# First pair of a token block: the two parts of a step's activation in neighbouring steps, and half of M1's passes behind the second product

## Chip, cores and metric

The kernel runs on one core of a Trainium2 chip. The metric is device microseconds of one execution; the time of the kernel before is the median of three runs. The core's engines work through queues of their own, each in the order in which it is written, and wait for each other by semaphores: TensorE (PE, with its weight loads PEld), VectorE (DVE), ScalarE (ACT), GpSimd (POOL) and SyncE (SP), which issues all DMAs here.

## What is computed

An attention over channels (256 by 256 scores, summed over 6016 tokens), then two feed-forward blocks, all in float32:

```python
def _attn_ref(q, k, v, tau):
    qn = q / (np.linalg.norm(q, axis=1, keepdims=True) + 1e-06)
    kn = k / (np.linalg.norm(k, axis=1, keepdims=True) + 1e-06)
    s = kn.transpose(0, 2, 1) @ qn / tau
    s = s - s.max(-1, keepdims=True)
    a = np.exp(s)
    a /= a.sum(-1, keepdims=True) + 1e-09
    return (v @ a).astype(np.float32)

def _moe_ref(x, w_in, w_out):          # d_model 256, d_ff 2048
    h = x @ w_in
    g = h * np.clip(h + 3.0, 0.0, 6.0) / 6.0
    return g @ w_out

def _moe2_ref(x, w_in, w_out):
    r = np.maximum(x @ w_in, 0.0)
    return (r * r) @ w_out
```

The weights come as 64-bit floats and are turned into float32 on the chip.

## The kernel before

**Precision.** A float32 operand is split into a high part (rounded to TensorE's fast float32 type, a cast on ScalarE, L124) and a low part (what is left, a subtraction on VectorE, L126; in places on GpSimd). A product is three passes: high by high, low by high, high by low. `split` does both parts, or one of them with `part` 0 or 1.

**Stages.** First the scores, norms and softmax. The attention is folded into the first feed-forward's weights: M1 is the attention matrix times w_in, made in four parts (c4, "part", 0 to 3) of 512 columns. Then come the tokens in six blocks ("pairs" of up to 512 columns each) through both feed-forwards. The first pair of the first feed-forward, `(0, 0)`, runs while weights are still being converted and M1 is still being made; it is written as 32 steps in plain products. All other pairs use a Strassen scheme planned by places (`strassen`, `prepare`, `at`, `extra`, `run`); the change doesn't touch them.

**A step of the first pair.** Step k is a token half n and a 128-wide slice f of the hidden layer, the list `steps`. TensorE makes tile h (six matmuls, `whole_product`, L311), ScalarE makes r = relu(h + 3) (L651), VectorE makes g = min(r, 6) * h (L653), ScalarE casts the high part gs of g (L124), VectorE makes its low part (L126), and TensorE adds the second product to the accumulators acc (six matmuls, `second_both`, L676): four use the high part, the last two the low part. `LAG` = 2: the second product of step k is written two steps later (`pending`, `drain`). The h tiles and M1's tiles mp take turns in four banks of PSUM (`bank`), so an h or mp tile waits for the g of the tile four turns back. Tile r and tile g have two buffers each, gs has four.

**What else goes through these queues.** `issue`, called inside `first` and at the end of a step, writes a stage of a weight's conversion (`unit`, `from_float64`: L155 and L158 on ScalarE, L159, L162 and L167 on VectorE, then `split`, whose cast and subtraction are L124 and L126 as well). Every eight steps a part of M1 is made: `m1_whole` (two halves i, six passes each, tile mp), in step 8p-3 for part p = 1, 2, 3. In step 8p-2 `m1_out` takes the halves out of PSUM as high parts (three instructions of L493 on ScalarE) and low parts (three of L495 on VectorE), which are the weights wa and a21 that h of step 8p is the first to use, and `m1_keep` copies both halves for sums that GpSimd makes later (L216, then L126 on GpSimd for parts 0 and 1). In step 8p-1 the second product of step 8p-3 is written ahead of h of step 8p (`late_products`), so that the weights have longer. GpSimd also makes combinations of the next pair's tokens (L752, L759).

**Order.** The code runs under `manual_schedule`: each engine's queue is in the order in which the code writes its instructions. So the order of lines in the loop over `steps` is the order in the queues.

Of the kernel before, what the change touches and what calls it, by code (L numbers as in the profile page):

```python
# [12 lines left out]
AF = mybir.ActivationFunctionType  # L13
ALU = mybir.AluOpType
# [7 lines left out]
KC = C // P  # L22
# [8 lines left out]
LAG = 2  # L31
# [25 lines left out]
def attention_then_two_ffns(  # L57
# [30 lines left out]
    nc = tc.nc  # L88
# [13 lines left out]
    def bank(shape, name, tag=None):  # L102

        if tag is None:
            tag = "yxyq"[turn[0] % 4]
            turn[0] += 1
        return ps_h.tile(shape, F32, tag=tag, name=name, bufs=2 if tag == "y" else 1)
# [6 lines left out]
    three = const.tile([P, 1], F32, name="three")  # L114
# [3 lines left out]
    def f32(x):  # L118
        return x.bitcast(F32)

    def split(hi, lo, x, part=2, eng=nc.vector):

        if part != 1:
            nc.scalar.copy(hi, x)  # L124
        if part != 0:
            eng.tensor_tensor(out=lo, in0=x, in1=f32(hi), op=ALU.subtract)  # L126
# [198 lines left out]
    with tc.manual_schedule():  # L325
# [10 lines left out]
        for gi, n in enumerate(GROUPS):  # L336
            src = wpool.tile([P, 1024], F32, tag=f"wo{gi % NU}", name=f"qk{gi}")[:, :2 * n * C]
            nc.sync.dma_start(
                out=src.rearrange("p (t x c) -> p t x c", t=n, x=2), in_=qk[:, t:t + n, :, :]
# [5 lines left out]
            if gi == TAU_AT:  # L345
# [4 lines left out]
                    out=tq[:, 2:4], in0=tq[:, 2:4], scalar1=tau_sb, scalar2=1.0, op0=ALU.mult, op1=ALU.mult  # L350
# [119 lines left out]
        def m1_whole(c4, i):  # L470
            mps[c4, i] = bank([P, 512], f"mp{c4}_{i}")
            low_last(mps[c4, i], [
                ([t[:, j, :] for t in wi1[c4]], [t[:, i, j * P:(j + 1) * P] for t in et]) for j in range(KC)
            ], False)
# [138 lines left out]
        def tmp(tag, w, name, **kw):  # L613
            return hpool.tile([P, WMAX], F32, tag=tag, name=name, **kw)[:, :w]

        def g_tile(w, name):
            t = gpool.tile([P, 2, WMAX], F32R, tag="g", name=name)[:, :, :w]
            return [t[:, i, :] for i in range(2)]


        w0 = WIDTHS[0]
        steps = [(n, f) for f in range(KF) for n in range(2)]
        steps[:4] = [(0, 0), (0, 1), (1, 0), (1, 1)]
        hs = {}
        pending = []
# [8 lines left out]
        def product(at, k):  # L634
            if at < len(steps):
                n, f = steps[at]
                if k == 0:
                    hs[at] = bank([P, WMAX], f"h0_{n}_{f}")[:, :w0]
                passes(hs[at], [(weight0(f, k), x0[k, n])], k == 0, k == KC - 1)

        def whole_product(at):
            if at < len(steps):
                n, f = steps[at]
                hs[at] = bank([P, WMAX], f"h0_{n}_{f}")[:, :w0]
                low_last(hs[at], [(weight0(f, k), x0[k, n]) for k in range(KC)])

        def first(at_step, between):
            n, f = steps[at_step]
            h = hs.pop(at_step)
            r = tmp("r", w0, f"r0_{n}_{f}")  # L650
            nc.scalar.activation(r, h, AF.Relu, bias=three)  # L651
            g = tmp("g32", w0, f"g0_{n}_{f}")
            nc.vector.scalar_tensor_tensor(out=g, in0=r, scalar=6.0, in1=h, op0=ALU.min, op1=ALU.mult)  # L653
            between()
            gs = g_tile(w0, f"gs0_{n}_{f}")
            if at_step == len(steps) - 1:
                at(1.6, lambda: split(*gs, g, 0))
                at(3.0, lambda: split(*gs, g, 1))
            else:
                split(*gs, g)  # L660
            return gs

        def second(n, f, gs):
            return [
# [16 lines left out]
        def drain(limit):  # L681
            while len(pending) > limit:
                second_both(*pending.pop(0))
# [9 lines left out]
        def issue():  # L693
            for k, st in sorted(plan.get(place[0], ())):
                loaded[k][st]()
                if st == 4:
                    feed()
            place[0] += 1
# [4 lines left out]
        def at(place, go):  # L703
            events.append((place, len(events), go))
# [12 lines left out]
        def run(until):  # L717
            events.sort(key=lambda e: e[:2])
            while events and events[0][0] < until:
                events.pop(0)[2]()  # L720
# [210 lines left out]
        for kk in range(KC):  # L931
            for a in range(2):
                product(a, kk)
        for a, (n, f) in enumerate(steps):
            gs = first(a, issue)
            pending.append((n, f, gs))

            part, since = divmod(a + M1_LEAD, 8)
            if 0 < part < 4 and since == 1:
                for i in range(KC):  # L940
                    m1_out(part, i)
                m1_keep(part)
            late_products = (a + 1) % 8 == 0 and a < 24
            if late_products:
                drain(LAG)
            if a:
                whole_product(a + 1)
            if 0 < part < 4 and since == 0:
                for i in range(KC):
                    m1_whole(part, i)  # L950
            drain(LAG)
            issue()

            run(-(len(steps) - 1 - a) * SLOTS / 4)


        for x, go in zip(LEFT_AT, [(n, f, d, gs) for n, f, gs in pending for d in range(KC)], strict=True):
            n, f, d, gs = go
# [48 lines left out]
```

## Time and profile before

| | |
|---|---|
| median of 3 runs | 1042.24 us (1042.06 to 1043.7) |
| profiled execution, its device time | 1042.34 us |
| its span | 1040.6 us |
| TensorE busy | 1031.6 us (99%), 4630 matmuls |
| VectorE busy | 852.5 us (82%) |
| ScalarE busy | 665.0 us (64%) |
| GpSimd busy | 28.9 us (3%) |

Matmuls are pipelined: one of 512 columns is listed with 0.39 us, though the next starts 0.23 us after it. So busy time says little of TensorE; what it loses is read from the distance between starts. The loop over the 32 steps begins at about 58 us of the span. In a listing a tile's name stands without its buffer number, `out<-in`; h is a first product of the first pair, mp a half of a part of M1, acc with L676 a second product of the first pair.

### The profile page before, as it was taken

How to read it: one execution, taken by the hardware profiler on the slowest of the kernel's cores; microseconds unless marked ns; L12 is line 12 of the kernel's file. 1: busy time of each engine (PE TensorE's matmuls, PEld its weight loads, DVE VectorE, ACT ScalarE, POOL GpSimd, SP SyncE). 2: the span in 40 equal slices, each digit the busy share in tenths (PEclk: the TensorE clock that was granted, in tenths of full speed). 3: DMA queues.
4: the chain of work that ended last, by engine and by line, in shares of the span. 5: the costliest groups of instructions: out<-in, count | busy, mean ns of one | idle time of the engine just before them, and what ended most of it. 6: DMA issues, size and time to landing. Idle time of an engine off the chain costs nothing.

```text
span 1040.6 us, 12968 instructions
## 1 busy us (share of the span) xinstructions
PE 1031.6 (99%) x4630; PEld 866.4 (83%) x4630; DVE 852.5 (82%) x1429; ACT 665.0 (64%) x1200; POOL 28.9 (3%) x33
## 2 busy tenths in 40 slices
PE   9999999999999999999999999999999999999998
PEld 8878788888888888888998888888888888888997
DVE  7898868889989889988988688688688688778765
ACT  6787777787788778877876445445445455445443
POOL 0012240000000000000000000000000000000000
PEclk9999999999999999999999999999999999999999
DMA  9911204003403403212755002002001100200100
GB/s 368 349 41 43 79 3 140 1 1 117 157 1 116 157 1 117 97 56 96 254 197 187 1 1 81 1 1 80 2 1 45 37 1 3 74 1 1 41 1 36
DMA packets 25936, 77.64 MB, mean 75 GB/s; under 512 B 2832, under 2 KB 4880, under 8 KB 25872
## 3 DMA queue, kind: packets, MB, share of 16 engines
q1 hardware_dynamic: 25872, 76.82, 20.9%
q8 instruction: 36, 0.59, 0.2%
q14 instruction: 28, 0.23, 0.1%
HBM read 52.95 MB, written 23.86 MB: 74 GB/s over the span
## 4 chain that ended last, share of the span: by engine, by line
PE 90%; DVE 3%; ACT 3%; DMA 2%; issue 1%; POOL 0%; ACTq 0%; SPq 0%; POOLq 0%
PE acc L323 15%; PE acc L321 15%; PE acc L322 15%; PE y L322 8%; PE y L321 8%; PE y L323 8%; PE q L321 4%; PE q L322 4%; PE q L323 4%; PE acc L676 2%; PE h L311 2%; PE x L321 2%; PE x L323 2%; PE x L322 2%; DMA qk<-in_qk 2%
## 5 line engine op out<-in xcount | busy, mean ns | idle before, releaser
L126 DVE TENSOR_TENSOR gs<-g,gs 128x512 fp32r<-128x512 f32 (+1 forms) x384 | 260.7, 679 | 59.8 <-ACT gs L828 47.8
L323 PE MATMUL acc<-gs,wo 128*128 128x512 f32 (+1 forms) x708 | 272.5, 385 | 0.1
L322 PE MATMUL acc<-gs,wo 128*128 128x512 f32 (+1 forms) x708 | 272.5, 385 | 0.0
L321 PE MATMUL acc<-gs,wo 128*128 128x512 f32 (+1 forms) x708 | 272.4, 385 | 0.0
L828 ACT CAST gs<-g 128x512 fp32r<-128x512 f32 (+1 forms) x352 | 208.1, 613 | 27.7 <-DVE g L819 19.0
L323 PEld LDWEIGHTS acc<-gs,wo 128*128 128x128 f32 x708 | 132.9, 188 | 25.3 <-DVE gs L126 0.5
L321 PEld LDWEIGHTS acc<-gs,wo 128*128 128x128 f32 x708 | 132.9, 188 | 24.4
L322 PEld LDWEIGHTS acc<-gs,wo 128*128 128x128 f32 x708 | 132.9, 188 | 24.3
L801 ACT COPY se<-y 128x512 f32<-128x512 f32 (+1 forms) x88 | 50.8, 577 | 124.0 <-PE y L323 123.9
L805 DVE TENSOR_TENSOR h<-q,se 128x512 f32<-128x512 f32 (+1 forms) x88 | 59.6, 678 | 65.6 <-ACT se L801 65.1
L801 ACT COPY su<-y 128x512 f32<-128x512 f32 (+1 forms) x88 | 50.9, 578 | 87.0 <-PE y L323 76.1
L824 DVE SCALAR_TENSOR_TENSOR g<-h 128x512 f32<-128x512 f32 (+1 forms) x144 | 97.0, 674 | 0.0
L811 ACT ACTIVATE r<-h,three 128x512 f32<-128x512 f32 (+1 forms) x120 | 85.5, 713 | 7.9 <-DVE h L805 7.7
L819 DVE SCALAR_TENSOR_TENSOR g<-r,h 128x512 f32<-128x512 f32 (+1 forms) x120 | 80.9, 674 | 3.9 <-ACT r L811 3.8
L813 ACT ACTIVATE r<-y 128x512 f32<-128x512 f32 (+1 forms) x48 | 28.3, 589 | 62.3 <-PE y L323 62.3
L805 DVE TENSOR_TENSOR h<-q,su 128x512 f32<-128x512 f32 (+1 forms) x88 | 59.5, 676 | 1.6
L805 DVE TENSOR_TENSOR h<-x,sa 128x512 f32<-128x512 f32 (+1 forms) x88 | 59.2, 673 | 0.0
L801 ACT COPY sa<-y 128x512 f32<-128x512 f32 (+1 forms) x88 | 50.8, 577 | 6.6 <-PE y L323 0.4
L824 DVE SCALAR_TENSOR_TENSOR g<-y,r 128x512 f32<-128x512 f32 (+1 forms) x48 | 32.7, 681 | 23.2 <-ACT r L813 22.7
L676 PE MATMUL acc<-gs,wo 128*128 128x512 f32 x180 | 45.5, 391 | 1.0 <-ACT gs L124 1.0
L300 PE MATMUL s<-qk 128*128 128x256 f32 x188 | 42.0, 385 | 0.0
L676 PEld LDWEIGHTS acc<-gs,wo 128*128 128x128 f32 x180 | 33.5, 188 | 9.1 <-ACT gs L124 2.2
(247 smaller groups left out, 1801.1 us busy)
## 6 DMA issues: line engine op xcount, KB each, us to landing
qk<-in_qk SPq DMA_DIRECT2D x23, 512.0 KB, 7.4
wo<-in_w_out SPq DMA_DIRECT2D x16, 512.0 KB, 5.1
wi<-in_w_in SPq DMA_DIRECT2D x10, 512.0 KB, 4.6
x2d<-o SPq DMA_DIRECT2D x20, 256.0 KB, 2.4
raw<-x2d SPq DMA_DIRECT2D x10, 512.0 KB, 5.8
out<-o SPq DMA_DIRECT2D x20, 256.0 KB, 2.2
raw<-in_vt SPq DMA_DIRECT2D x8, 512.0 KB, 5.9
wo2d<-wo2s SPq DMA_DIRECT2D x8, 512.0 KB, 2.9
```

Source lines behind the costliest of these rows:

```text
L126: eng.tensor_tensor(out=lo, in0=x, in1=f32(hi), op=ALU.subtract)
L300: nc.tensor.matmul(s_ps[i], lhsT=x[:, C + i * P:C + (i + 1) * P], rhs=x[:, :C], start=(t == 0), stop=(t == NT - 1))
L321: nc.tensor.matmul(ps, lhsT=ah, rhs=bh, start=first, stop=False, skip_group_check=more)
L322: nc.tensor.matmul(ps, lhsT=al, rhs=bh, start=False, stop=False, skip_group_check=more)
L323: nc.tensor.matmul(ps, lhsT=ah, rhs=bl, start=False, stop=last, skip_group_check=more)
L676: nc.tensor.matmul(acc[0, 0, n, d], lhsT=wo1[u][:, i, at + d * P:at + (d + 1) * P], rhs=gs[k], start=f == 0 and (i, k) == (0, 0), stop=f = ...
L801: nc.scalar.copy(s[tag], s["y"])
L805: nc.vector.tensor_tensor(out=s[which], in0=s[ps], in1=s[tag], op=ALU.add)
L811: nc.scalar.activation(s["r" + which], h, AF.Relu, bias=three)
L819: nc.vector.scalar_tensor_tensor(out=g, in0=s["r" + which], scalar=6.0, in1=h, op0=ALU.min, op1=ALU.mult)
L824: nc.vector.scalar_tensor_tensor(out=g, in0=h, scalar=0.0, in1=r, op0=ALU.max, op1=ALU.mult)
L828: nc.scalar.copy(gs[which][0], s["g" + which])
```

## The change

Four things, all in the loop over `steps`:

- r of step k+1 is written in step k, behind that step's new product and ahead of everything else that ScalarE does in step k (`relu0`). In the steps with `late_products` it is written behind the high part of step k.
- the product of step k+1 is written at the head of step k (it stood behind the step's r, g and parts); in the order of TensorE's own queue this moves nothing.
- the low part of a step (`part0(a - 1, 1)`) is written one step later than its high part, behind the next step's g, conversion stage and high part.
- of M1's two halves the second is written behind `drain`, so the second product of step 8p-5 lies between the halves.

The number of instructions on each engine stays as it was.

```diff
--- before.py
+++ after.py
@@ -644,21 +644,27 @@
                 hs[at] = bank([P, WMAX], f"h0_{n}_{f}")[:, :w0]
                 low_last(hs[at], [(weight0(f, k), x0[k, n]) for k in range(KC)])
 
-        def first(at_step, between):
+        rs, gs0 = {}, {}
+
+        def relu0(at_step):
+            if at_step < len(steps):
+                n, f = steps[at_step]
+                rs[at_step] = tmp("r", w0, f"r0_{n}_{f}")
+                nc.scalar.activation(rs[at_step], hs[at_step], AF.Relu, bias=three)
+
+        def gate0(at_step):
             n, f = steps[at_step]
-            h = hs.pop(at_step)
-            r = tmp("r", w0, f"r0_{n}_{f}")
-            nc.scalar.activation(r, h, AF.Relu, bias=three)
             g = tmp("g32", w0, f"g0_{n}_{f}")
-            nc.vector.scalar_tensor_tensor(out=g, in0=r, scalar=6.0, in1=h, op0=ALU.min, op1=ALU.mult)
-            between()
-            gs = g_tile(w0, f"gs0_{n}_{f}")
-            if at_step == len(steps) - 1:
-                at(1.6, lambda: split(*gs, g, 0))
-                at(3.0, lambda: split(*gs, g, 1))
-            else:
-                split(*gs, g)
-            return gs
+            nc.vector.scalar_tensor_tensor(
+                out=g, in0=rs.pop(at_step), scalar=6.0, in1=hs.pop(at_step), op0=ALU.min, op1=ALU.mult
+            )
+            gs0[at_step] = g_tile(w0, f"gs0_{n}_{f}"), g
+            return gs0[at_step][0]
+
+        def part0(at_step, part):
+            if at_step >= 0:
+                (hi, lo), g = gs0.pop(at_step) if part else gs0[at_step]
+                split(hi, lo, g, part)
 
         def second(n, f, gs):
             return [
@@ -931,24 +937,36 @@
         for kk in range(KC):
             for a in range(2):
                 product(a, kk)
+        relu0(0)
         for a, (n, f) in enumerate(steps):
-            gs = first(a, issue)
-            pending.append((n, f, gs))
-
             part, since = divmod(a + M1_LEAD, 8)
+            late_products = (a + 1) % 8 == 0 and a < 24
+            if late_products:
+                drain(LAG - 1)
+            if a:
+                whole_product(a + 1)
+            if not late_products:
+                relu0(a + 1)
+            pending.append((n, f, gate0(a)))
+            issue()
+            if a == len(steps) - 1:
+                at(1.6, lambda: part0(len(steps) - 1, 0))
+                at(3.0, lambda: part0(len(steps) - 1, 1))
+            else:
+                part0(a, 0)
+            if late_products:
+                relu0(a + 1)
+            part0(a - 1, 1)
             if 0 < part < 4 and since == 1:
                 for i in range(KC):
                     m1_out(part, i)
                 m1_keep(part)
-            late_products = (a + 1) % 8 == 0 and a < 24
-            if late_products:
-                drain(LAG)
-            if a:
-                whole_product(a + 1)
-            if 0 < part < 4 and since == 0:
-                for i in range(KC):
-                    m1_whole(part, i)
+            m1 = 0 < part < 4 and since == 0
+            if m1:
+                m1_whole(part, 0)
             drain(LAG)
+            if m1:
+                m1_whole(part, 1)
             issue()
 
             run(-(len(steps) - 1 - a) * SLOTS / 4)
```

VectorE's queue at the first steps, before (g_n_f is tile g of a step, gs its parts; tawi, wi1l and tawo are weights being converted; L167 is listed as ISA here and as CUSTOM_DVE in the trace):

```order
L653 SCALAR_TENSOR_TENSOR g_0_0_588<-r_0_0_586,h_0_0_572 128x512
L167 ISA tawi_2_536<-tawi_2_536,tywi_2_538 128x1024
L126 TENSOR_TENSOR gs_0_0_595<-g_0_0_588,gs_0_0_595 128x512
L126 TENSOR_TENSOR wi1l_599<-tawi_2_536,wi1h_598 128x512
L159 TENSOR_SCALAR tawo_1_591<-wo_1_432 128x512
L653 SCALAR_TENSOR_TENSOR g_0_1_608<-r_0_1_606,h_0_1_576 128x512
L162 SCALAR_TENSOR_TENSOR tawo_1_591<-tbwo_1_592,tawo_1_591 128x512
L126 TENSOR_TENSOR gs_0_1_611<-g_0_1_608,gs_0_1_611 128x512
```

and in the changed kernel:

```order
L658 SCALAR_TENSOR_TENSOR g_0_0_590<-r_0_0_586,h_0_0_572 128x512
L167 ISA tawi_2_536<-tawi_2_536,tywi_2_538 128x1024
L126 TENSOR_TENSOR wi1l_600<-tawi_2_536,wi1h_599 128x512
L159 TENSOR_SCALAR tawo_1_594<-wo_1_432 128x512
L658 SCALAR_TENSOR_TENSOR g_0_1_616<-r_0_1_588,h_0_1_576 128x512
L162 SCALAR_TENSOR_TENSOR tawo_1_594<-tbwo_1_595,tawo_1_594 128x512
L126 TENSOR_TENSOR gs_0_0_592<-g_0_0_590,gs_0_0_592 128x512
```

The low part of step 0 (gs_0_0) stood directly behind L167 and ahead of the weights' low part; now it stands behind the weights' low part, L159, g of step 1 and L162.

ScalarE's queue in steps 5 and 6, where part 1 of M1 is taken out (steps 6 and 7 are n, f = 0, 3 and 1, 3; r_1_3 is r of step 7), before:

```order
L651 ACTIVATE r_0_3_754<-h_0_3_725,three 128x512
L158 ACTIVATE tywi_4_712<-raw13h 128x512
L124 CAST gs_0_3_760<-g_0_3_756 128x512
L493 ACTIVATE wa_1h<-mp_0_732,rs_504 128x2x128
L493 ACTIVATE a_1_765<-mp_0_732,rs_504 128x256
L493 ACTIVATE wa_1h<-mp_1_739,rs_518 128x2x256
L503 ACTIVATE m_11_772<-mp_0_732,rs_504 128x512
L503 ACTIVATE m_11_772<-mp_1_739,rs_518 128x512
L155 ACTIVATE tbwo_3_790<-wo_3_682 128x512
L651 ACTIVATE r_1_3_794<-h_1_3_775,three 128x512
```

and in the changed kernel:

```order
L653 ACTIVATE r_0_3_722<-h_0_3_715,three 128x512
L124 CAST wo_2_727<-tawo_2_669 128x512
L124 CAST gs_1_2_726<-g_1_2_724 128x512
L653 ACTIVATE r_1_3_762<-h_1_3_755,three 128x512
L158 ACTIVATE tywi_4_713<-raw13h 128x512
L124 CAST gs_0_3_766<-g_0_3_764 128x512
L493 ACTIVATE wa_1h<-mp_0_733,rs_504 128x2x128
L493 ACTIVATE a_1_773<-mp_0_733,rs_504 128x256
L493 ACTIVATE wa_1h<-mp_1_746,rs_518 128x2x256
L503 ACTIVATE m_11_780<-mp_0_733,rs_504 128x512
L503 ACTIVATE m_11_780<-mp_1_746,rs_518 128x512
L155 ACTIVATE tbwo_3_791<-wo_3_683 128x512
```

r of step 7 stood behind the eviction casts (wa_1h, a_1) and the copies (m_11) of part 1; now it stands ahead of them, and ahead of the cast of step 6.

TensorE's queue at the two halves of part 1 (mp_0 and mp_1; eth and etl are the attention's parts), before:

```order
L311 MATMUL mp_0_732<-wi1l_599,eth 128x512 x2
L311 MATMUL mp_1_739<-wi1h_598,eth 128x512
L311 MATMUL mp_1_739<-wi1h_598,etl 128x512
L311 MATMUL mp_1_739<-wi1h_598,eth 128x512
L311 MATMUL mp_1_739<-wi1h_598,etl 128x512
L311 MATMUL mp_1_739<-wi1l_599,eth 128x512 x2
L676 MATMUL acc_0_1_0_701<-gs_1_1_664,wo_0_499 128x512 x2
```

and in the changed kernel:

```order
L311 MATMUL mp_0_733<-wi1l_600,eth 128x512 x2
L682 MATMUL acc_0_1_0_702<-gs_1_1_667,wo_0_499 128x512 x2
L682 MATMUL acc_0_1_1_703<-gs_1_1_667,wo_0_499 128x512 x2
L682 MATMUL acc_0_1_0_702<-gs_1_1_667,wo_0_499 128x512
L682 MATMUL acc_0_1_1_703<-gs_1_1_667,wo_0_499 128x512
L311 MATMUL mp_1_746<-wi1h_599,eth 128x512
L311 MATMUL mp_1_746<-wi1h_599,etl 128x512
L311 MATMUL mp_1_746<-wi1h_599,eth 128x512
L311 MATMUL mp_1_746<-wi1h_599,etl 128x512
L311 MATMUL mp_1_746<-wi1l_600,eth 128x512 x2
```

The second product of step 3 (acc_0_1 from gs_1_1) stood behind both halves; now it stands between them.

## Rows read from the trace of the kernel before

**Rows 1.** Windows: start:end, length, busy us (count) of PE, PEld, DVE, ACT, POOL, PEclk, DMA, GB/s.
```profile
139.00:1030.00 891.00, 891.00 (x4004) 751.32 (x4003) 731.86 (x1224) 556.60 (x1006) 9.42 (x7) 1.00 0.17 60
```

**Rows 2.** Timeline of PE, first pair: start us, us, instruction, count, idle before.
```profile
58.59 1.07 PE L311 MATMUL h<-x,wa_0h 128*128 128x512 f32 x4
...
61.31 1.52 PE L676 MATMUL acc<-gs,wo 128*128 128x512 f32 x6
...
72.20 0.50 PE L311 MATMUL mp<-wi1h,eth 128*128 128x512 f32 x1 [0.63 <-DVE g L653]
...
76.42 2.88 PE L676 MATMUL acc<-gs,wo 128*128 128x512 f32 x12
...
95.45 0.39 PE L311 MATMUL mp<-wi1h,eth 128*128 128x512 f32 x1
...
115.27 1.54 PE L676 MATMUL acc<-gs,wo 128*128 128x512 f32 x6
...
119.16 1.65 PE L676 MATMUL acc<-gs,wo 128*128 128x512 f32 x6 [0.96 <-ACT gs L124]
...
133.56 1.52 PE L676 MATMUL acc<-gs,wo 128*128 128x512 f32 x6
```

**Rows 3.** Waits from 58 to 141 us: who for whom, total us, times, longest.
```profile
ACT gs L124 <- DVE g L653: 15.2, 24, 1.5
DVE g L653 <- ACT r L651: 6.8, 8, 1.3
```

**Rows 4.** Timeline of DVE at the first steps.
```profile
59.50 1.18 DVE L167 CUSTOM_DVE_ANT_0 tawi<-tawi,tywi 128x1024 uint16<-128x1024 uint16 x1
...
61.76 0.68 DVE L126 TENSOR_TENSOR wi1l<-tawi,wi1h 128x512 fp32r<-128x512 f32 x1
62.36 0.41 DVE L159 TENSOR_SCALAR tawo<-wo 128x512 int32<-128x512 int32 x1
62.69 0.67 DVE L653 SCALAR_TENSOR_TENSOR g<-r,h 128x512 f32<-128x512 f32 x1
63.29 0.68 DVE L162 SCALAR_TENSOR_TENSOR tawo<-tbwo,tawo 128x512 int32<-128x512 int32 x1
64.05 0.69 DVE L126 TENSOR_TENSOR gs<-g,gs 128x512 fp32r<-128x512 f32 x1
```

**Rows 5.** Timeline of ACT there, the cast that VectorE's wi1l needs.
```profile
60.71 0.62 ACT L124 CAST wi1h<-tawi 128x512 fp32r<-128x512 f32 x1 [0.48 <-DVE tawi L167]
```

**Rows 6.** Timeline of ACT where part 1 of M1 is taken out.
```profile
75.29 0.68 ACT L651 ACTIVATE r<-h,three 128x512 f32<-128x512 f32 x1
75.88 0.65 ACT L158 ACTIVATE tywi<-raw13h 128x512 int32<-128x512 uint32 x1
76.75 0.62 ACT L124 CAST gs<-g 128x512 fp32r<-128x512 f32 x1 [0.22 <-DVE g L653]
77.27 0.47 ACT L493 ACTIVATE wa_1h<-mp,rs 128x256 fp32r<-128x256 f32 x1
77.64 0.47 ACT L493 ACTIVATE a<-mp,rs 128x256 fp32r<-128x256 f32 x1
78.00 0.69 ACT L493 ACTIVATE wa_1h<-mp,rs 128x512 fp32r<-128x512 f32 x1
```

**Rows 7.** Timeline of DVE there, the last low part of the new weights.
```profile
78.94 0.74 DVE L495 SCALAR_TENSOR_TENSOR wa_1l<-mp,rs,wa_1h 128x512 fp32r<-128x512 f32 x1
```

**Rows 8.** Timeline of POOL: a low part and two of the sums.
```profile
89.78 1.29 POOL L126 TENSOR_TENSOR wa_0l<-m,wa_0h 128x512 fp32r<-128x512 f32 x1 [1.80 <-ACT wa_0h L124]
91.03 0.93 POOL L216 TENSOR_TENSOR m<-m 128x256 f32<-128x256 f32 x1
92.04 1.07 POOL L216 TENSOR_TENSOR m<-m,m 128x256 f32<-128x256 f32 x1
```

**Rows 9.** Timeline of DVE beside these sums.
```profile
91.70 0.81 DVE L126 TENSOR_TENSOR gs<-g,gs 128x512 fp32r<-128x512 f32 x1 [0.34 <-ACT gs L124]
92.43 1.23 DVE L162 SCALAR_TENSOR_TENSOR tawi<-tbwi,tawi 128x512 int32<-128x512 int32 x1
```

## The prediction

> **What bounds it now.** I read the windows first: from 139 us to 1030 us TensorE is busy for all of 891 us [rows 1], so whatever the first pair loses or gains ahead of that is carried to the end one to one, and nothing behind it can give it back. Then TensorE's listing over the first pair [rows 2]. I count in blocks of six matmuls: P(k), the first product of step k (tile h), S(k), its second product (tile acc), and the six passes of one half of a part of M1 (tile mp). From 76.42 to 95.45 there are 14 blocks in 19.03 us: 1.36 us a block, 0.227 us a matmul. With that pace the other stretches show what is lost now: 58.59 to 76.42 holds 12 blocks (16.32) and took 17.83, so 1.51 us; 95.45 to 115.27 holds 14 (19.04) and took 19.82, so 0.78; 115.27 to 133.56 holds 12 (16.32) and took 18.29, so 1.97. **4.26 us of waits in all**, the largest at 72.20 (second half of M1's passes, waiting for a g on VectorE, since that g frees its bank) and 119.16 (a high part not yet cast). That is the most the change can win. Last the waits [rows 3]: ScalarE stood 15.2 us for g, and VectorE 6.8 us for r, because r, g, high and low of a step chase each other between two queues. VectorE is not idle otherwise; in the first stretch its instructions follow each other 0.6 us apart [rows 4].
>
> **What the change removes.** TensorE's blocks are the same ones in the same order, but for the second half of M1's passes, which now has S(8p-5) ahead of it (p is the part of M1, 1 to 3). The bank's g gets 1.36 us more, which is more than each of the three waits there (0.63 at the first by its row), so they go. The wait at 119.16 came from ScalarE and VectorE running late around GpSimd's work; with r a step ahead the 15.2 and 6.8 us of chasing mostly go, so I take this out too. Nothing is added in instructions: ScalarE, VectorE and GpSimd run what they ran. I set the whole 4.26 us as removed and look for what is late instead, following the new order with the old durations.
>
> **First new wait: the low part of step 0.** It stood directly behind L167 on VectorE and covered ScalarE's cast of the weights; now the low part of the weights stands there and must wait for that cast. L167 ends at 59.50 + 1.18 = 60.68 [rows 4], the cast runs 60.71 to 61.33 [rows 5], VectorE goes on at 61.36: weights' low part 0.60, L159 0.33, g of step 1 0.60, L162 0.60 (start to start, [rows 4]), and then low part of step 0 with 0.69, done at 64.18. TensorE starts S(0) at 61.31 [rows 2] and asks for the low part four matmuls later, at 62.22. That is 2.0 us, and 0.1 more, since six matmuls behind a stop take 1.65 us against 1.52 [rows 2]: **2.1 us**. The low part of step 1 is seven places on in the same full queue, at 67.1, just when S(1), moved by 2.1 us, asks for it: 0.2 us. What hid this before was that the low part came before the next conversion.
>
> **Second new wait: M1's eviction.** In step 8p-2 ScalarE now has r of step 8p-1 ahead of that step's cast and of the three casts that make the weights for P(8p). That r needs P(8p-1). Counted from the start of P(8p-1): its result 1.52 [rows 2], hand over 0.07, r 0.59, L158 0.56 (0.65 less the overlap of about 0.1 with which casts follow each other), cast 0.52, first weights 0.37, second 0.36, third 0.69 [rows 6]: 4.68. P(8p) starts three blocks after P(8p-1), at 4.08, and wants the third weights two matmuls later, at 4.53: 0.2 late with the hand over, and 0.1 for the stop. The low parts follow on VectorE: the last ends 79.68 where the second weights were cast at 78.11 [rows 6, 7], 1.57 later; here 4.10 + 1.57 = 5.67, wanted at about 5.5: 0.2 and 0.1 again. **0.6 us, three times, 1.8 us**. Before, these casts stood ahead of that r and needed no product of their step. VectorE idles too: by the same count its queue is done at 76.5 and waits for the casts until 80.0 at the first of them.
>
> **Third: GpSimd, now that there is no slack.** Where a VectorE instruction with two inputs in SBUF meets a running GpSimd instruction, it ends 0.55 us after that one: 91.03 + 0.93 = 91.96, and the low part of 91.70 ends at 92.51; 92.04 + 1.07 = 93.11, and L162 of 92.43 ends at 93.66 [rows 8, 9]. In the stretch without lost time (76.42 to 95.45) this costs TensorE nothing now. After the 3.5 idle us the low parts are just in time: low parts of steps 6 and 7 come out only 0.1 to 0.2 us before they are asked for. Following the queues from 80.0 (twelve instructions and a wait of 0.6 us for a cast), L167 of the third w_out unit comes up at 87.87, while the cast that releases GpSimd's 1.29 us [rows 8] ends at 87.55. GpSimd goes first by 0.24 us, runs from 87.63 to 88.92, L167 ends at 89.47, low part of step 8 at 90.07; S(8) asks at 89.63: 0.6 us with the stop. The second such GpSimd instruction and the four sums behind it hold VectorE in the same way, which makes the low parts of steps 9 and 10 late by 0.7 us each: **2.0 us**. Behind the second part of M1 the same happens with GpSimd's next pair, at step 16: **1.4 us**.
>
> **Sum.** Added 2.1 + 0.2 + 1.8 + 2.0 + 1.4 = 7.5, removed 4.26: 3.3 us slower. The profiled execution took 1042.34 us (span 1040.6), by 0.1 above the median of three, 1042.24. 1042.34 + 3.3 = **1045.6 us**.
>
> **Bounds of the unknown costs.** The first two waits follow from the order alone, and I trust them to a few tenths. The third hangs on margins of a quarter of a microsecond. It may be nothing (sum 4.1 - 4.26 = -0.1), or also catch steps 17, 18 and 22, where the same count leaves no more slack, for another 0.3 to 2 us. I take the middle since the nearest rows, 91.70 and 92.43, show the hold each time the two met.
>
> **Rivals.** *Removed against added, and no more* (0.27): VectorE's instruction comes up before GpSimd's, or the low parts have more slack than I count. Then 1042.2 us, or with one of the four collisions 1043. The rows cannot tell who is first within 0.24 us. The Trainium skill bears on this (SBUF — State Buffer, Who interferes with whom): which of the two blocks the other is decided by who issues first, and the loser stands for the whole instruction. By that rule the four collisions become GpSimd's wait wherever VectorE is first, and the time is this rival's; the trace agrees on the blocking (0.55 us after the end), no run here shows the other order. *Worse* (0.16): the low parts of 17, 18 and 22 are caught too, or misses of 0.1 us at steps 6, 7, 14, 15 add up: 4.5 to 6 us, 1046.8 to 1048.3. *Faster* (0.10), the other side: r a step ahead takes the 15.2 and 6.8 us of chasing out of both queues, VectorE gets so far ahead that M1's casts and the low parts are never asked for too early, and only the wait of step 0 stays: 4.26 - 2.3 = 2.0 us less, 1040.3 us; 1038.1 if even that is covered. It decides at VectorE's lead over TensorE: 2.0 us more at S(0), where 62.22 is asked and 64.18 counted, would do. Against it: r now waits for a product that TensorE has just made, so neither queue can run ahead by more than a step. That the change does not do what it says is out: the order shows each move.
>
> **Chances.** My forecast 0.47, the rivals 0.27, 0.16 and 0.10. A measurement of this kernel tells some 0.2% (2.1 us) from no change. Slower by more than that: most of the forecast and all of the worse, 0.60. Within it: most of the first rival, and the part of the forecast with only one or two collisions, 0.30. Faster: 0.10. The range leaves out the faster case and the far end of the worse: 1042.0 to 1047.6 us; the likeliest case's own range is 1044.3 to 1046.8.
>
> **What the profile after would show.** A gap of about 2 us in the first S block at about 62, its release a VectorE low part (L126). Three times 0.4 to 0.7 us in the first P block of a new part of M1, released by the casts and low parts of M1's eviction, and VectorE idle for 3 us ahead of each. No wait any more in the mp blocks. Waits for low parts in S(8) to S(10) and S(16), with VectorE instructions of 1.2 us and more beside GpSimd's ahead of them. From 140 us on no gap. I am wrong if S(0) is not held, if M1's casts come before r in time, or if the waits for low parts are missing.

## The result, and the profile after

The changed kernel takes 1049.51 us (median of 5 runs, 1047.93 to 1050.49) against 1042.06 (5 runs, 1041.79 to 1043.7): ratio 1.0067, 95% interval 1.0056 to 1.0078. It is slower by 0.7%, which the prediction had as the likelier sign, but by 7.1 to 7.5 us where it said 3.3, and outside the range that it gave (up to 1047.6). The execution profiled after is the one of 1049.51, with a span of 1047.7; that is 7.1 us more than before.

I line the two traces up by the start of the same block of matmuls, and call the difference the lag. It is 0.14 us where the loop over the steps begins and 5.97 where the pair of 448-column products begins, at 475 us of before: **5.8 us are lost in the first pair**. Another 1.2 us arise inside that one pair, far from the change; I come back to them.

TensorE's timeline of the changed kernel, the starts of second products (tile acc) on which it stood (start, us, instruction, count, idle before and its release):

```profile
61.45 1.07 PE L682 MATMUL acc<-gs,wo 128*128 128x512 f32 x4
64.39 0.73 PE L682 MATMUL acc<-gs,wo 128*128 128x512 f32 x2 [1.87 <-DVE gs L126]
...
77.43 2.88 PE L682 MATMUL acc<-gs,wo 128*128 128x512 f32 x12
80.15 1.39 PE L311 MATMUL h<-x,wa_1h 128*128 128x512 f32 x4
...
90.33 0.73 PE L682 MATMUL acc<-gs,wo 128*128 128x512 f32 x2 [0.28 <-DVE gs L126]
...
93.71 0.73 PE L682 MATMUL acc<-gs,wo 128*128 128x512 f32 x2 [0.34 <-DVE gs L126]
...
97.20 0.73 PE L682 MATMUL acc<-gs,wo 128*128 128x512 f32 x2 [0.47 <-DVE gs L126]
...
118.57 0.73 PE L682 MATMUL acc<-gs,wo 128*128 128x512 f32 x2 [1.36 <-DVE gs L126]
...
122.31 0.73 PE L682 MATMUL acc<-gs,wo 128*128 128x512 f32 x2 [0.73 <-DVE gs L126]
...
140.28 0.72 PE L682 MATMUL acc<-gs,wo 128*128 128x512 f32 x2 [0.70 <-DVE gs L126]
```

A block of six now breaks behind its fourth matmul: the two that need the low part stand alone and carry the idle time. These seven are S(0), S(8), S(9), S(10), S(16), S(17) and S(22). The idle number is less than what a wait costs, since the matmul ahead is listed with 0.39 us while the next could start after 0.227. The cost is read from starts: at S(0) 64.39 stands where 61.45 + 4 x 0.227 = 62.36 was due, so 2.03, and 0.11 more until the next block, 2.14 together. The row at 80.15 is the first product with new weights: its four matmuls are listed with 1.39 us instead of 1.07, without an idle time of their own; the next block starts 1.98 us after it (at 82.14) instead of 1.36. Of the waits of before [rows 2], the one at 72.20 is gone: the two halves of M1 start at 71.99 and 74.71 and wait for nothing.

Who waited for whom, first pair, in the changed kernel (total us, times, longest; GpSimd's own waits and smaller ones are left out):

```profile
ACT r L653 <- PE h L311: 10.7, 5, 3.3
ACT gs L124 <- DVE g L658: 9.3, 14, 2.0
PEld acc L682 <- DVE gs L126: 9.0, 8, 2.3
PE acc L682 <- DVE gs L126: 5.8, 7, 1.9
DVE wa_3l L495 <- ACT a L493: 3.5, 1, 3.5
DVE wa_1l L495 <- ACT a L493: 3.4, 1, 3.4
DVE wa_2l L495 <- ACT a L493: 3.4, 1, 3.4
...
DVE g L658 <- ACT r L653: 0.9, 1, 0.9
```

The chasing did shrink: ScalarE's wait for g fell from 15.2 to 9.3 us and VectorE's for r from 6.8 to 0.9 [rows 3]. In its place VectorE stands three times for 3.4 us, and TensorE itself stands for low parts.

Behind the first pair TensorE is again without a gap (window from 141 to 1030 us: length, then busy us of PE, PEld, DVE, ACT, POOL, then PEclk, DMA, GB/s), as [rows 1] was, and at full granted clock:

```profile
141.00:1030.00 889.00, 889.00 (x3987) 747.86 (x3986) 730.13 (x1218) 554.54 (x1002) 11.08 (x8) 1.00 0.18 61
```

### Where the three kinds of wait are seen

VectorE at the first steps of the changed kernel, to be held against [rows 4]:

```profile
59.63 1.18 DVE L167 CUSTOM_DVE_ANT_0 tawi<-tawi,tywi 128x1024 uint16<-128x1024 uint16 x1
61.50 0.69 DVE L126 TENSOR_TENSOR wi1l<-tawi,wi1h 128x512 fp32r<-128x512 f32 x1 [0.69 <-ACT wi1h L124]
...
63.65 0.68 DVE L126 TENSOR_TENSOR gs<-g,gs 128x512 fp32r<-128x512 f32 x1
```

The place of the low part behind L167 is now 0.69 us of idle time, and the low part of step 0 ends at 64.33, where 64.18 was forecast.

ScalarE, then VectorE, where part 1 of M1 is taken out:

```profile
77.69 0.69 ACT L653 ACTIVATE r<-h,three 128x512 f32<-128x512 f32 x1 [3.26 <-PE h L311]
78.28 0.65 ACT L158 ACTIVATE tywi<-raw13h 128x512 int32<-128x512 uint32 x1
78.83 0.61 ACT L124 CAST gs<-g 128x512 fp32r<-128x512 f32 x1
79.34 0.48 ACT L493 ACTIVATE wa_1h<-mp,rs 128x256 fp32r<-128x256 f32 x1
79.70 0.47 ACT L493 ACTIVATE a<-mp,rs 128x256 fp32r<-128x256 f32 x1
80.06 0.70 ACT L493 ACTIVATE wa_1h<-mp,rs 128x512 fp32r<-128x512 f32 x1
```
```profile
76.14 0.69 DVE L126 TENSOR_TENSOR gs<-g,gs 128x512 fp32r<-128x512 f32 x1
80.21 0.48 DVE L495 SCALAR_TENSOR_TENSOR wa_1l<-mp,rs,wa_1h 128x256 fp32r<-128x256 f32 x1 [3.39 <-ACT a L493]
```

These are the rows of [rows 6, 7] with r in front. ScalarE stands 3.26 us for the product that r needs, and the casts behind it need none; VectorE stands 3.39 us behind those casts.

GpSimd, then VectorE's instructions beside it, at steps 8 to 10, 16, 17 and 22:

```profile
87.83 1.29 POOL L126 TENSOR_TENSOR wa_0l<-m,wa_0h 128x512 fp32r<-128x512 f32 x1 [26.42 <-ACT wa_0h L124]
...
92.18 0.93 POOL L216 TENSOR_TENSOR m<-m 128x256 f32<-128x256 f32 x1
...
114.99 2.98 POOL L126 TENSOR_TENSOR wa_1l<-m,wa_1h 128x512 fp32r<-128x512 f32 x2 [18.40 <-ACT wa_1h L124]
...
120.35 1.36 POOL L758 TENSOR_TENSOR t<-raw,t 128x512 f32<-128x512 f32 x1
138.04 1.64 POOL L765 TENSOR_TENSOR x<-raw,x 128x512 fp32r<-128x512 f32 x1 [16.33 <-ACT x L761]
```
```profile
88.07 1.61 DVE L167 CUSTOM_DVE_ANT_0 tawo<-tawo,tywo 128x1024 uint16<-128x1024 uint16 x1
...
92.43 1.23 DVE L126 TENSOR_TENSOR gs<-g,gs 128x512 fp32r<-128x512 f32 x1
...
116.76 1.76 DVE L126 TENSOR_TENSOR gs<-g,gs 128x512 fp32r<-128x512 f32 x1
...
120.48 1.78 DVE L126 TENSOR_TENSOR gs<-g,gs 128x512 fp32r<-128x512 f32 x1
...
137.85 0.68 DVE L167 CUSTOM_DVE_ANT_0 tawo<-tawo,tywo 128x1024 uint16<-128x1024 uint16 x1
138.45 1.78 DVE L126 TENSOR_TENSOR gs<-g,gs 128x512 fp32r<-128x512 f32 x1
```

Each VectorE instruction here but the one of 137.85 ends 0.55 us after the GpSimd instruction that runs beside it: 92.18 + 0.93 = 93.11 and 92.43 + 1.23 = 93.66; 120.35 + 1.36 = 121.71 and 122.26; 138.04 + 1.64 = 139.68 and 140.23. At step 8 GpSimd comes first by 0.24 us (87.83 against 88.07), which is the margin that the prediction counted.

### The profile page after: what moved, and what is told of

Read it like the earlier page. It is cut to its first block, busy times and chain, and to the rows that moved or that the text cites. A ratio compares the mean times of both kernels' runs of the same rounds, so it can differ in the third digit from the quotient of the medians.

```text
span 1047.7 us, 12978 instructions
## 1 busy us (share of the span) xinstructions
PE 1034.9 (99%) x4630; PEld 866.1 (83%) x4630; DVE 855.7 (82%) x1429; ACT 664.4 (63%) x1200; POOL 30.9 (3%) x33
## 4 chain that ended last, share of the span: by engine, by line
PE 91%; DVE 4%; ACT 3%; issue 1%; DMA 1%; POOL 0%; ACTq 0%; DVEq 0%; SPq 0%; POOLq 0%
PE acc L323 15%; PE acc L322 15%; PE acc L321 15%; PE y L322 7%; PE y L323 7%; PE y L321 7%; PE q L323 4%; PE q L322 4%; PE q L321 4%; PE acc L682 2%; PE h L311 2%; PE x L323 2%; PE x L321 2%; PE x L322 2%; PE s L300 1%
## 5 line engine op out<-in xcount | busy, mean ns | idle before, releaser
L126 DVE TENSOR_TENSOR gs<-g,gs 128x512 fp32r<-128x512 f32 (+1 forms) x384 | 265.3, 691 | 52.7 <-ACT gs L834 48.1
```

## Experiments

The last column is the change of the lag over the first pair, against before, in one execution of each kernel; the two executions of the changed kernel differ by 0.4 us in it, so smaller differences between rows say little. Behind the first pair TensorE loses nothing but what is told at the end.

| kernel | median us | ratio, 95% interval | first pair, us |
|---|---|---|---|
| before (four sets of runs) | 1042.06 to 1042.35 | 1 | 0 |
| after | 1049.51 | 1.0067, 1.0056 to 1.0078 | +5.8 |
| after_again | 1049.11 | 1.0069, 1.0056 to 1.0081 | +6.2 |
| a_m1_only | 1042.03 | 1.0003, 0.9994 to 1.0012 | +0.1 |
| f_low_later | 1045.14 | 1.0025, 1.0015 to 1.0034 | +1.4 in the fastest execution |
| b_low_back | 1041.78 | 0.9996, 0.9986 to 1.0005 | -0.6 |
| c_evict_first | 1043.1 | 1.0009, 0.9999 to 1.0018 | +0.7 |
| e_both_back | 1041.96 | 0.9998, 0.9989 to 1.0007 | -0.6 |
| h_m1_back | 1042.23 | 1.0, 0.9991 to 1.0009 | -0.6 |
| i_later_unit | 1042.54 | 1.0002, 0.9993 to 1.001 | -0.1 |
| j_conv_shift | 1041.5 | 0.9994, 0.9985 to 1.0003 | -1.4 |
| d_pool_writes | 1042.17 | 1.0001, 0.9991 to 1.001 | -0.1 |
| d1_sums_write | 1044.65 | 1.0022, 1.0013 to 1.0031 | +1.9 |
| d2_tokens_write | 1045.54 | 1.0038, 1.0024 to 1.0051 | +3.8 |

### One part alone, or one part undone

**a_m1_only**: before, with only the half of M1's passes moved.

```diff
-            if 0 < part < 4 and since == 0:
-                for i in range(KC):
-                    m1_whole(part, i)
+            m1 = 0 < part < 4 and since == 0
+            if m1:
+                m1_whole(part, 0)
             drain(LAG)
+            if m1:
+                m1_whole(part, 1)
```

> The kernel before with one part of the change alone: the second half of M1's passes stands behind the second product. My theory: this is the part that gains. The three waits of that half for a bank (about 0.95, 0.56 and 0.5 us with what lies around them) go, nothing takes their place, and the time is 1.5 to 2 us under the kernel before, about 1040.3 us. Rival: the second product that now comes earlier, or the eviction that now has its half later, takes the wait over, and the time stays at 1042.

It gains nothing that can be measured. The wait of [rows 2] at 72.20 is gone and stands one block further on, in P(7), for the g that frees its bank (TensorE's timeline; the second row is the wait that [rows 2] has at 119.16):

```profile
74.33 0.73 PE L311 MATMUL h<-x,a 128*128 128x512 f32 x2 [0.48 <-DVE g L653]
...
119.54 0.72 PE L676 MATMUL acc<-gs,wo 128*128 128x512 f32 x2 [0.70 <-DVE gs L126]
```

That g runs on VectorE from 73.60 to 74.28, in a queue with hardly any idle time. So the moved passes change who waits, not how late VectorE is.

**b_low_back**: after, with the low part directly behind its high part again.

```diff
                 part0(a, 0)
+                part0(a, 1)
             if late_products:
                 relu0(a + 1)
-            part0(a - 1, 1)
```

> The changed kernel with one part undone: the low part stands directly behind its high part again; r a step ahead and M1's halves stay. My theory: the wait at step 0 (2.1 us) goes, and so do the waits for low parts at steps 8, 9, 10, 16, 17 and 22 (together some 6 us), since each low part comes one step earlier; the three waits for M1's eviction (0.6 us each) stay. About 8 us under the changed kernel, 1041 to 1043 us. Rival: the low parts are late because VectorE stood 3.4 us at each of M1's evictions, not because they are written a step later; then only the 2.1 us of step 0 go, and it is about 1047 us.

As expected: the wait in S(0) is gone and with it every wait at steps 8 to 22. The three evictions still cost 0.6 us each. That leaves a kernel that cannot be told from before. **Undoing the low part's place alone gives back all that was lost.**

**f_low_later**: before, with the low part alone a step later.

```diff
+        lows = []
 ...
             between()
 ...
+                if at_step:
+                    lows.pop()()
 ...
-                split(*gs, g)
+                split(*gs, g, 0)
+                if at_step:
+                    lows.pop()()
+                lows.append(lambda: split(*gs, g, 1))
```

> The kernel before with one part of the change alone: each low part is written one step later, behind the next step's high part; r stays in its own step, M1's halves stay together. If a low part a step later costs by itself, the 2 us of step 0 come in full, and waits for low parts beside GpSimd at some of the steps 8, 9, 10, 16 and 17: 4 to 6 us over the kernel before, 1046 to 1048 us. If those late low parts need VectorE's standing at the evictions, which r ahead brings, only step 0 costs, less what the kernel before already waited in the first steps: 1043 to 1044 us.

It costs 2.6 us by the ratio, between the two expectations. S(0) costs 2.4 us, and S(10), S(16) and S(17) cost 0.75 to 1.2, though VectorE stands only 0.5 us at each eviction. Yet none of the large waits of before is left: S(18), which had waited 0.96 us at 119.16 [rows 2], runs through. TensorE's timeline, S(0) and S(18):

```profile
63.67 0.73 PE L683 MATMUL acc<-gs,wo 128*128 128x512 f32 x2 [2.10 <-DVE gs L126]
...
120.59 1.52 PE L683 MATMUL acc<-gs,wo 128*128 128x512 f32 x6
```

The profiled execution is the fastest of its ten (1043.02 to 1046.14), so its +1.4 is the low end.

**c_evict_first**: after, with r of the next step behind the eviction in the steps 8p-2.

```diff
-            if not late_products:
+            out_now = 0 < part < 4 and since == 1
+            if not late_products and not out_now:
                 relu0(a + 1)
 ...
                 m1_keep(part)
+                relu0(a + 1)
```

> The changed kernel with another part undone: in the three steps that take M1's halves out, r of the next step stands behind that eviction again; low parts stay a step later. If the late low parts come from VectorE's 3.4 us of standing at the evictions, both the eviction's waits (1.8 us) and those at steps 8, 9, 10, 16, 17 and 22 (6 us) go, and only step 0 (2.3 us) stays: about 1042 us. If they come from being written a step later, beside GpSimd's work, only 1.8 us go, and it is about 1047.5 us.

The three eviction waits go, and VectorE's standing in front of them falls from 3.4 to 0.5 us each. So do S(8) and S(22). But S(0) stays, and so does a part of the collisions. TensorE's timeline:

```profile
63.48 0.73 PE L682 MATMUL acc<-gs,wo 128*128 128x512 f32 x2 [1.88 <-DVE gs L126]
94.55 0.73 PE L682 MATMUL acc<-gs,wo 128*128 128x512 f32 x2 [0.48 <-DVE gs L126]
114.21 0.73 PE L682 MATMUL acc<-gs,wo 128*128 128x512 f32 x2 [0.33 <-DVE gs L126]
117.96 0.73 PE L682 MATMUL acc<-gs,wo 128*128 128x512 f32 x2 [0.73 <-DVE gs L126]
```

At steps 9, 10, 16 and 17 they add up to 2.5 us, where steps 8 to 22 of after have 5.5. **So some 3 us of the collisions come from VectorE's lead lost behind r, and 2.5 from the low part being late by itself.** It lies between the two theories.

**e_both_back**: both edits, b and c, which leaves r a step ahead and M1's half moved.

> Both parts that cost are undone: the low part stands behind its high part, and in the three steps that take M1's halves out r of the next step stands behind that eviction; r a step ahead in all other steps and M1's second half behind the second product stay. My theory, that the three costs add up and are independent: the evictions' 0.6 us each go from the run with only the low part back (1041.8 us), and what stays is some 1.3 us of waits in the first eight steps against 4.26 us in the kernel before: 2.5 to 3 us under the kernel before, 1039.2 to 1039.7 us. Rival: with r later at the evictions the low parts behind them get late and meet GpSimd again, as in the run with only the eviction undone (2.5 us of such waits): 1041.5 us or more.

My expectation fell: I had taken the 4.26 us of waits of before as gone, and 0.6 came. This is TensorE's timeline there:

```profile
74.71 0.74 PE L311 MATMUL h<-x,a 128*128 128x512 f32 x2 [0.26 <-DVE g L658]
119.46 0.73 PE L682 MATMUL acc<-gs,wo 128*128 128x512 f32 x2 [0.55 <-DVE gs L126]
```

With smaller ones at P(15), P(16), P(23), P(24), S(1) and S(2) and in M1's passes there are some 3.4 us of waits. The rival's time came, but of its waits for low parts only the one at S(18). Against b_low_back the three eviction waits of 0.6 us are gone, but S(18) waits again, and the first pair is no shorter. ScalarE still stands 14.3 us for g. The wait in S(18) is for a low part that ran 1.78 us, from 117.62 to 119.40, beside GpSimd's 1.36 us from 117.49. r a step ahead did not remove that.

**h_m1_back** (e with the halves of M1 together) and **i_later_unit** (e with the fifth conversion begun two places, which is one step, later):

```diff
-START = [-5, -3, 0, 3, 6] + [9 + 4 * k for k in range(9)]
+START = [-5, -3, 0, 3, 8] + [9 + 4 * k for k in range(9)]
```

> As the run with both costs undone, but with M1's two halves next to each other again, so r a step ahead is all that is left of the change. In the kernel before with only the halves moved, the gain was 0.2 us, since the next product then waited for a bank in place of the half. If the halves gain only once r is ahead, this is 0.8 to 1.5 us slower than the run with both undone. If r a step ahead brings g in time by itself, the two are equal within 0.3 us.

> As the run with both costs undone, and the conversion of the third w_out unit begins two places (one step) later, so VectorE has three instructions fewer ahead of g of steps 4 and 5. If the 0.5 us that the product of step 7 waits for the bank of g of step 5 comes from VectorE's queue in the dense first steps, it goes: 0.3 to 0.6 us under the run with both undone, about 1038.9 us. Rival: the unit then lands on VectorE at the eviction of M1's first part and costs there what it saves: no difference.

With the halves together their wait is back (0.75, 0.49 and 0.43 us), the ones at P(7), P(15) and P(23) are gone, and the time is the same. The later conversion takes the wait from P(7) and puts 0.7 us into P(8). Both times the wait changes its place only. I read it as VectorE's queue being full there, so that whichever block is next in need pays.

**j_conv_shift** spreads the later conversions away from GpSimd's work.

```diff
-START = [-5, -3, 0, 3, 6] + [9 + 4 * k for k in range(9)]
+START = [-5, -3, 0, 3, 6, 9, 13, 17, 21, 25, 35, 30, 40, 44]
```

> The run with both costs undone, and four conversions moved: the last w_in unit three places earlier, the last three w_out units later, so no conversion's instructions are on VectorE at steps 18 and 19, where GpSimd makes combinations of the next pair's tokens. There the run with both undone still waited 0.95 us for a low part. If that wait is VectorE's queue meeting GpSimd, it goes: 0.7 to 1 us less than that run, 1041.0 to 1041.3 us. If GpSimd alone makes it, it stays; if the w_out units come too late, a new wait stands at step 20's second product.

The first pair gains 1.4 us, but S(18) still costs 0.7; against e_both_back the gain is at P(23) to P(25), which no longer wait, and not where it was looked for. The interval (0.9985 to 1.0003) holds no change. No version was found that beats the kernel before.

### GpSimd's part

**d_pool_writes**, **d1_sums_write** and **d2_tokens_write** are the changed kernel with GpSimd's subtractions and sums turned into writes of zeros, which read nothing: all of them, only those on M1's sums and low parts, and only those on the next pair's tokens.

```diff
-            return nc.gpsimd if first else nc.vector
+            return writes_only if first else nc.vector
+
+        class writes_only:
+            @staticmethod
+            def tensor_tensor(out, in0, in1, op):
+                nc.gpsimd.memset(f32(out) if out.dtype == F32R else out, 0.0)
```

> The changed kernel in which GpSimd's 23 additions and subtractions in the first pair are replaced by instructions that fill the same tiles with zeros and read nothing, so what follows is computed from wrong weights and wrong tokens; the order of all queues is the same. My theory: the waits for low parts at steps 8, 9, 10, 16, 17 and 22 come from VectorE standing behind GpSimd's reads; they go (some 6 us), while step 0 (2.1 us) and the evictions (1.8 us) stay: about 1043.5 us, with the first pair's lag over the kernel before down to 0. Rival: VectorE's own queue makes them late, GpSimd adds little: over 1047 us.

> The changed kernel in which twelve of GpSimd's 23 instructions of the first pair, those on M1's sums and their low parts (parts 0 and 1), fill their tiles with zeros and read nothing, so the weights are wrong; the eleven on the next pair's tokens are as they were. If each wait for a low part comes from the GpSimd instruction that runs beside it, the waits at steps 8, 9, 10 and 16 go (0.55, 0.6, 0.75 and 1.65 us, 3.5 together), and those at 17 and 22 (1.0 each) stay: 1044.5 to 1046 us. If VectorE is late by itself and the collisions only add up, the waits at 9, 10 and 16 shrink but stay, over 1046.5 us.

> The counterpart: the eleven GpSimd instructions on the next pair's tokens write zeros and read nothing (wrong tokens for that pair), the twelve on M1's sums are as they were. By my theory the waits at steps 17 and 22 go (2 us), and those at 8, 9, 10 and 16 stay (3.5 us): 1046 to 1047.5 us. With the run before this one the two amounts add up to what the run without any GpSimd reads gained, about 6 us. Rival: the waits at 17 and 22 are what is left of 16's; then they stay.

With all of them the waits at 8, 9, 10, 16, 17 and 22 are gone, and one row is left of TensorE's waits for low parts:

```profile
63.60 0.74 PE L687 MATMUL acc<-gs,wo 128*128 128x512 f32 x2 [1.60 <-DVE gs L126]
```

The first pair is 5.9 to 6.3 us shorter than in after and after_again, more than I expected (1043.5). S(0) and the evictions stay, and what they cost is paid for by the waits of before that went, of which S(18), beside GpSimd too, is one. **So the low part a step later and the 3.4 us of standing cost the first pair its 6 us only together with GpSimd's work beside them.** With M1's writes only, the waits at 8, 9, 10 and 16 go, S(17) gives place to one of 1.0 us in S(18), and S(22) stays; with the tokens' only, 17 and 22 go and the others stay:

```profile
89.27 0.73 PE L687 MATMUL acc<-gs,wo 128*128 128x512 f32 x2 [0.29 <-DVE gs L126]
92.66 0.73 PE L687 MATMUL acc<-gs,wo 128*128 128x512 f32 x2 [0.37 <-DVE gs L126]
96.14 0.73 PE L687 MATMUL acc<-gs,wo 128*128 128x512 f32 x2 [0.47 <-DVE gs L126]
117.51 0.73 PE L687 MATMUL acc<-gs,wo 128*128 128x512 f32 x2 [1.36 <-DVE gs L126]
```

Against the mean of after and after_again (6.0) they give back 4.1 and 2.2 us, together 6.3, where both at once give 6.1: the two groups of waits are separate.

The Trainium skill (SBUF — State Buffer, Who interferes with whom) says that a VectorE instruction with two inputs in SBUF contends with a GpSimd instruction that reads SBUF, not with one that only writes. The runs agree, in few places: the memsets of d_pool_writes need no operands and run earlier, so at steps 8 to 10 none is beside VectorE any more. Where a low part did meet one it was not held: that of 115.85 took 0.69 us beside the memset of 115.82 (0.58 us), and ended 0.14 us after it.

### The same kernel once more

**after_again** is the changed kernel, unchanged.

> The changed kernel once more, beside its parts and with more runs. The profile of it showed 5.8 us of loss in the first pair and 1.2 us more in the first feed-forward's last pair, where the 448-column matmuls started 208.5 ns apart and not 205.4. My theory: that second amount has nothing to do with the change. Then the times fall into two heaps some 1.2 us apart, near 1048 and 1049.3 us, and this profile shows the first pair's 5.5 to 6 us again, with or without the other 1.2. Rival: the change brings both; then every profile of it shows the 208.5 ns, and none of the times lies near 1048.

The waits are at the same places with the same sizes within 0.1 us, but for S(17) with 1.3 instead of 1.0. The last 1.2 us are not there. Of the five times, 1047.9, 1048.2 and 1049.11 lie near the two heaps expected; 1050.63 and 1051.16 lie above both, and what they add is in no trace. The 1.2 us lie in the pair of 448-column products, of which a window from 500 to 550 us counts the matmuls: before (a row not shown ahead), after, and after_again:

```profile
500.00:550.00 50.00, 50.00 (x248) 46.27 (x247) 44.16 (x81) 37.79 (x72) 0.00 (x0) 1.00 0.60 208
```
```profile
500.00:550.00 50.00, 50.00 (x244) 45.42 (x243) 44.66 (x83) 38.59 (x74) 0.00 (x0) 1.00 0.68 234
```
```profile
500.00:550.00 50.00, 50.00 (x248) 46.34 (x248) 45.51 (x85) 38.66 (x75) 0.00 (x0) 1.00 0.70 234
```

244 matmuls against 248 in the same 50 us, without a gap and at the same clock. In the longest row of 448-column matmuls, 318 of them, the starts are 206.5 ns apart in after and 202.8 in after_again, which makes the 1.2 us. (The 208.5 and 205.4 ns of the expectation are means over 403 matmuls of the pair, 43 of which have 512 columns.) Since the code is the same, it is not the change.

## Why the prediction was wrong in its size

**The first new wait** was right: S(0) cost 2.14 us (2.1 forecast), S(1) 0.17 (0.2).

**The second** was right: P(8), P(16) and P(24) cost 0.62 each by their starts (0.6 forecast). VectorE stood 3.4 us ahead of each, at the place and for the reason given; c_evict_first shows the reason.

**The third, GpSimd without slack, is the step that failed, as a term that was mis-sized.** Forecast were 3.4 us; 5.5 came. That is 2.1 of the 2.5 us by which the first pair lost more than the 3.3 forecast; the pace of the 448-column products puts 1.2 us on top in the execution profiled, but 1042.34 + 5.8 alone is over 1047.6 already.

| | S(8) | S(9) | S(10) | S(16) | S(17) | S(22) |
|---|---|---|---|---|---|---|
| forecast, us | 0.6 | 0.7 | 0.7 | 1.4 | 0 | 0 |
| measured, us | 0.55 | 0.63 | 0.74 | 1.63 | 1.0 | 0.97 |

The four that were followed through the queues are right to a quarter of a microsecond. Steps 17 and 22 were seen, left to the rival "worse" with a price of 0.3 to 2 us, and left out of the sum; they came with 2.0. Step 18, named with them, did not wait. The sum followed the queues from one known collision to the next and stopped where the margin became small, instead of carrying them on.

**The 4.26 us removed** were nearly right in size: 2.14 + 0.17 + 1.87 + 5.5 = 9.7 added and 5.8 lost leave 3.9 removed, and in the trace of after neither S(2) nor a second half of M1 nor S(18) waits any more. But the reason was not the one given. They do not go because r is a step ahead: e_both_back has r ahead, none of the new waits of S(0) or of the evictions, and is only 0.6 us ahead of before. Nor is r ahead or the moved half needed: f_low_later has neither, and these waits are gone there too. I read it so: where TensorE is held by the new waits, it asks later for what it waited for before. b_low_back and e_both_back bear this out, since they differ by three waits of 0.62 us, 1.87 together, and their first pairs are equal (both 0.6 us ahead of before). For the first steps it is argued: every kernel that lost the waits of S(2) and of the second half of M1's part 1 (or of the product behind it) has its low parts a step later and also stands 1.9 to 2.4 us at S(0), so no run tells the new order on VectorE from TensorE's being held. Then removed and added are largely two names for one queue's lateness, and as separate terms they came out near by luck. The claim that M1's passes gain by 1.36 us more for their bank is refuted as a gain: a_m1_only and h_m1_back against e_both_back change nothing.

**The rivals.** "Removed against added, and no more" fell, since GpSimd was first at step 8, by just the margin counted. Nor would VectorE first have been free. The prediction says that no run shows that order, but step 22 does: VectorE's L167 of 137.85 came first and took its 0.68 us, GpSimd's instruction behind it took 1.64 us where that of 87.83 took 1.29, and the low part behind that one was held until 140.23. The trace of before has such a case too, a GpSimd instruction of 1.75 us at 143.15, begun while VectorE's low part of 142.56 (1.19 us) ran. "Faster" fell with e_both_back: even without the new waits the order gains nothing measurable. That VectorE's amount of work sets this is my reading and not tried by itself. "Worse" named the right steps; its price of 4.5 to 6 us holds the 5.8 of the first pair. Its upper time of 1048.3 is still under the median by 1.2 us, as much as the other pair's pace, which no step of mine had.

**What was wrong in the chances**: the rows of before showed the hold each time GpSimd and VectorE met, so a case in which it strikes four times and then not at 17 and 22, with no slack left there, deserved less than the 0.47 it got, and "worse" more than 0.16.

## What to carry to other kernels

A part that is moved later in a full in-order queue takes everything that was written between with it: ask not whether it is due a step later, but what now stands ahead of it, and which of these waits for another engine. An instruction that waits for a product just issued holds all work behind it that needs none; put it behind that work, even where it is "ahead" by a step. When the queue that feeds TensorE has no slack, follow each collision on to the end of the stage, since a wait that is moved or removed only comes out at the next block.

## What the runs showed that I had not expected

- GpSimd is busy for 3% of the span, and its work costs the changed kernel 6 us: a low part that comes up behind a GpSimd subtraction or sum ends 0.55 us after it in the rows shown, and takes 1.2 to 1.8 us there where it takes 0.68 alone.
- The hold goes both ways: a GpSimd instruction that VectorE's L167 preceded ended 1.15 us after L167 (step 22) and held the next low part the longer.
- A break in TensorE's row costs 0.11 us beyond the wait itself, at each place where it was read.
- In the first feed-forward's last pair the 318 matmuls of 448 columns in a row ran at 202.7 to 202.9 ns each in ten of the fourteen profiled executions and at 206.5 in four (after, d_pool_writes, d1_sums_write, j_conv_shift), at the same granted clock; the second such pair, near the end, at 203.8 to 203.9 in all. The same kernel showed both. What selects the pace stays open.
